# Attention with packed keys and a softplus feed-forward on one core: one subtraction of the weight conversion moves from VectorE to GpSimd

## The chip, the cores and the metric

The kernel runs on one core of one Trainium2 chip. The metric is the device time of an execution in microseconds (us), as a median over runs. The core's engines run side by side, each through its own instruction list in order, and meet through semaphores: TensorE (PE in the profile), VectorE (DVE), ScalarE (ACT), GpSimd (POOL) and SyncE (SP), which issues the DMA transfers.

## The reference

There are eight batches of eight heads, 576 tokens, head width 64. In each batch and head, 32 "pack" queries attend over the 576 keys and values, and then the 576 queries attend over the 32 packed rows. The result, 4608 x 512, goes through a feed-forward block of width 2048 with a softplus between its two products:

```
s = scale * q @ k.T ; a = softmax(s)            # scale = 1/8, head by head
p_packed = attn(p, k, v)                        # 32 x 64 for each head
x   = attn(q, p_packed, p_packed)               # 576 x 64 for each head
h   = x @ w_in                                  # 4608 x 512 by 512 x 2048
g   = max(h, 0) + log1p(exp(-|h|))              # softplus
out = g @ w_out                                 # 4608 x 2048 by 2048 x 512
```

`w_in` and `w_out` arrive as 64-bit floats; all else is 32-bit.

## The kernel before, in words

**The feed-forward products.** Each big product is done with a high and a low word for both factors, as three matmuls: high by high, high by low, low by high. For one batch `b` and one slice `f` of 128 of the 2048 hidden columns, `gemm1` (L497) makes the hidden values in two PSUM tiles `ph` of 288 tokens. `softplus` takes them through ScalarE (|h|, exp, log: L523, L524, L525 into `e`), VectorE (the sum with max(h, 0): L528), GpSimd (L534, 64 left-over tokens into `rest`), and VectorE again (`gh` and `gl`, the high and low words: L513, L514). Two slices later `gemm2_tile` (L541) multiplies them with `wo_h` and `wo_l`, the high and low words of `w_out`. One slice of one batch is called a unit here; batch 0 is units 0 to 15. Only two `ph` tiles and two `e` tiles exist, so TensorE can start the next unit's L497 only when VectorE's L528 has read the old `ph`.

**Attention** of the next batch is cut into small steps and threaded between these matmuls: transposes on TensorE whose results ScalarE copies out of PSUM (`T_k`, `T_q` at L245, `a1T` at L286), scores (L252), VectorE's softmax parts (L327 to L343), and the high and low words of the attention weights (`at_h` L442, `at_l` L443). `make_m` (L460, tiles `psm`, for each second slice of batch 0) multiplies the packed rows with two slices of `w_in`; ScalarE and VectorE split its result into `mh` and `ml` (L475, L476). These small PSUM tiles share two banks in turn, so the second half of an L460 group can begin only when the copy out of the tile before it but one has been made.

**The weight conversion** (`convert`) turns the 64-bit weights into 32-bit ones while batch 0 runs. There are 32 elements of 128 x 512 numbers; elements 4p and 4p+1 are slices 2p and 2p+1 of `w_in`, 4p+2 and 4p+3 the same slices of `w_out`. Each element takes two ScalarE passes (`m` L174, `r` L178), two on VectorE (`t`: L180, L185) and an integer add on GpSimd (L193). For `w_in` that add writes the weight where it is used. For `w_out` it writes back into `t`; ScalarE then rounds it to the high word `wo_h` (L212), and the line of the change makes the low word `wo_l = t - wo_h` (L218). There are two buffers for each of `t` and `r` and one for `m` once batch 0's units run, so element n+2 reuses the `t` of element n: for a `w_out` element that `t` comes free when L218 has read it.

**What sets the order.** TensorE's list stands as the code writes it. The lists of the other engines are arranged by a scheduler ahead of time, so that a changed engine for one operation also moves others around it. On the chip each list is then worked off strictly in order.

Of the kernel before, what the change touches and what calls it, by code (L numbers as in the profile page):

```python
# [26 lines left out]
def pack_attention_then_softplus_ffn(  # L27
# [10 lines left out]
    nc = tc.nc  # L38
# [87 lines left out]
    def load64(srcs, nm, tag="x"):  # L126
        pool, bufs = (cv, 2) if tag == "x" else (work, 1)
        x = pool.tile([P, CN], I64, tag=tag, name=f"x_{nm}", bufs=bufs)
        n = P // len(srcs)
        for i, src in enumerate(srcs):  # L130
            nc.sync.dma_start(
                x[i * n:(i + 1) * n].rearrange("x (a n) -> x a n", a=src.shape[1]), src
            )
        return x
# [13 lines left out]
    def convert(order):  # L148

        srcs = {"i": w_in_src, "o": w_out_src}

        slots = ["x", "x", "at_h", "at_l"]
        xs, ts, rs = {}, {}, {}

        def prefetch(n):
            if n < len(order):
                w, i = order[n]
                xs[n] = load64(srcs[w](i), f"{w}{i}", slots[n % 4] if n < 8 else "x")  # L160

        def first(n):
            x = xs.pop(n)
            lo = x.bitcast(U32).rearrange("x (n two) -> x n two", two=2)[:, :, 0]
            hi = x.bitcast(F32).rearrange("x (n two) -> x n two", two=2)[:, :, 1]
            pool, tm, tr, tt = (work, "gh", "gl", "gh") if spare and n % 2 else (cv, "m", "r", "t")

            m = pool.tile([P, CN], F32, tag=tm, name=f"m_{n}", bufs=LAG + 1 if pool is work else 1)
            nc.scalar.mul(m, hi, 2.0**-112)  # L174


            r = pool.tile([P, CN], I32, tag=tr, name=f"r_{n}", bufs=LAG + 1 if pool is work else 2)
            nc.scalar.activation(r, lo, AF.Copy, scale=2.0**-29)  # L178
            t = pool.tile([P, CN], I32, tag=tt, name=f"t_{n}", bufs=LAG + 1 if pool is work else 2)
            nc.vector.tensor_scalar(t, m.bitcast(I32), -0x80000000, None, op0=ALU.bitwise_and)  # L180
            ts[n], rs[n] = (t, m), r

        def second(n):
            t, m = ts[n]
            nc.vector.scalar_tensor_tensor(  # L185
                t, m.bitcast(I32), 3, t, op0=ALU.logical_shift_left, op1=ALU.bitwise_or
            )
            w, i = order[n]
            dst, a = t, 1
            if w == "i":  # L190
                dst, a = w_in_sb.bitcast(I32)[:, :, i * P:(i + 1) * P], DM // P
            v = [y.rearrange("x (a n) -> x a n", a=a) for y in (t, rs.pop(n))]
            nc.gpsimd.tensor_tensor(  # L193
                dst if a > 1 else dst.rearrange("x (a n) -> x a n", a=a), *v, op=ALU.add
            )

        for n in range(2):
            prefetch(n)
        yield
        for n in range(2, 4):  # L200
            prefetch(n)
        yield
        for n in range(len(order) + 1):
            if n < len(order):
                first(n)
                if n < 6 or n >= 8:
                    prefetch(n + 4 if n < 6 else n + 2)
            yield
            w, i = order[n - 1] if n else ("i", 0)
            t = ts.pop(n - 1)[0].bitcast(F32) if n else None  # L210
            if w == "o":
                nc.scalar.copy(wo_h[:, i, :], t)  # L212
            yield
            if n < len(order):
                second(n)
            yield
            if w == "o":
                nc.vector.tensor_tensor(  # L218
                    wo_l[:, i, :], t, wo_h[:, i, :].bitcast(F32), op=ALU.subtract
                )  # L220
                yield
# [370 lines left out]

    pt = load_pack(0, (nc.sync, nc.scalar))
    conv = convert(order)
    for g in range(G):
        load("k", 0, g)
# [104 lines left out]
```

## Time and profile before

| What | Value |
|---|---|
| time, median of 3 runs | 799.0 us (796.33, 799.0, 799.79) |
| profiled execution, first to last instruction | 794.2 us |
| what lies around that span, by the median | 4.8 us |
| TensorE busy | 766.6 us, 97% of the span |
| VectorE, ScalarE, GpSimd busy | 511.3, 464.8, 94.2 us |
| conversion's work on the three engines | from 12.9 to 138 us of the span |
| L218, the line of the change | 16 instructions on VectorE, 12.5 us together |

The page gives no separate time for the profiled execution itself, so its span stands beside the median. A row of a group names line, engine, operation, output and inputs with shapes and count; then busy time and mean of one; then idle time of the engine just before, and what ended it. A row of a timeline has start, duration, engine, line, operation, and in brackets the engine's idle time before it with what ended that. In a row of windows each engine's busy time is followed by the number of its instructions, and the granted clock of TensorE is a share of full speed.

### The profile page before, as it was taken

The page shows a single profiled execution, that of the slowest core. Times are in us where ns is not written, and L with a number is a line of the kernel's source. Part 1 is how long each engine was busy: PE and PEld are TensorE (multiplying, and loading weights), DVE is VectorE, ACT ScalarE, POOL GpSimd, SP SyncE. Part 2 cuts the span into 40 slices and gives each one's busy share as a digit, 9 for nine tenths or more (in the row PEclk, how much of TensorE's full clock was granted, in tenths as well). Part 3 has the DMA queues.
Part 4 walks back from the last instruction along what each step waited for, and adds up shares of the span by engine and source line. Part 5 has one row for each costly group of instructions (what it writes and reads, how often), then busy time and mean ns, then how long its engine had stood idle before and what let it go on. Part 6 is the DMA issues. An engine that isn't in the chain of part 4 may idle for free.

```text
span 794.2 us, 14986 instructions
## 1 busy us (share of the span) xinstructions
PE 766.6 (97%) x5724; PEld 609.0 (77%) x5724; DVE 511.3 (64%) x1168; ACT 464.8 (59%) x1181; POOL 94.2 (12%) x166
## 2 busy tenths in 40 slices
PE   6879988999999999999999999999999999999997
PEld 4656766877788787877788787887888777778886
DVE  2788899754686547765677447764677546765554
ACT  5769887665662755665554555665555465555540
POOL 1415353000000000000000000000000000000010
PEclk9999999999999999999999999999999999999999
DMA  9977784031213121032213112132211210010002
GB/s 229 248 188 178 172 229 112 8 107 31 61 31 83 45 56 48 18 83 61 61 31 84 26 50 60 31 84 61 61 31 42 56 31 2 1 54 1 1 0 67
DMA packets 38216, 56.02 MB, mean 71 GB/s; under 512 B 4864, under 2 KB 31488, under 8 KB 38144
## 3 DMA queue, kind: packets, MB, share of 16 engines
q1 hardware_dynamic: 37600, 54.93, 27.2%
q8 instruction: 45, 0.74, 0.4%
q14 instruction: 27, 0.22, 0.1%
q10 hardware_dynamic: 544, 0.13, 0.1%
HBM read 45.61 MB, written 9.44 MB: 69 GB/s over the span
## 4 chain that ended last, share of the span: by engine, by line
PE 80%; ACT 0%; DVE 0%; issue 0%; ACTq 0%; DVEq 0%
PE acc L541 40%; PE ph L497 23%; PE acc_m L541 6%; PE psm L460 3%; PE ps L252 2%; PE psT_q L239 2%; PE psT_k L239 2%; PE psp L295 1%; PE psa L285 1%; PE psx L308 0%; PE ppt L105 0%; ACT e L525 0%; ACT e L524 0%; ACT e L523 0%; DVE o L550 0%; DVE o_m L550 0%
## 5 line engine op out<-in xcount | busy, mean ns | idle before, releaser
L528 DVE SCALAR_TENSOR_TENSOR e<-ph,e 128x288 f32<-128x288 f32 x256 | 114.5, 454 | 167.5 <-ACT e L525 166.2
L541 PE MATMUL acc<-wo_h,gh 128*128 128x512 f32 x512 | 214.8, 419 | 0.7 <-DVE o L550 0.7
L541 PE MATMUL acc<-wo_l,gh 128*128 128x512 f32 x512 | 201.6, 394 | 0.0
L541 PE MATMUL acc<-wo_h,gl 128*128 128x512 f32 x512 | 201.5, 394 | 0.0
L523 ACT ACTIVATE e<-ph 128x288 f32<-128x288 f32 x256 | 103.0, 403 | 163.1 <-PE ph L497 110.7
L497 PE MATMUL ph<-at_h,mh 128*128 128x288 f32 x512 | 159.0, 311 | 5.4 <-DVE e L528 4.5
L497 PE MATMUL ph<-at_l,mh 128*128 128x288 f32 x512 | 152.2, 297 | 1.4 <-DVE at_l L443 1.2
L497 PE MATMUL ph<-at_h,ml 128*128 128x288 f32 x512 | 152.2, 297 | 0.0
L497 PEld LDWEIGHTS ph<-at_h,mh 128*128 128x128 f32 x512 | 96.8, 189 | 40.0 <-DVE gl L514 14.1
L534 POOL COPY rest<-e 128x64 f32<-128x64 f32 x128 | 47.3, 369 | 599.3 <-DVE e L528 598.5
L541 PEld LDWEIGHTS acc<-wo_h,gh 128*128 128x128 f32 x512 | 96.4, 188 | 23.1 <-issue 9.8
L541 PEld LDWEIGHTS acc<-wo_h,gl 128*128 128x128 f32 x512 | 96.4, 188 | 21.7
L524 ACT ACTIVATE e<-e 128x288 f32<-128x288 f32 (+1 forms) x240 | 109.2, 455 | 3.5
L525 ACT ACTIVATE e<-e 128x288 f32<-128x288 f32 (+1 forms) x240 | 109.7, 457 | 2.0
L541 PEld LDWEIGHTS acc<-wo_l,gh 128*128 128x128 f32 x512 | 96.9, 189 | 9.8
L497 PEld LDWEIGHTS ph<-at_l,mh 128*128 128x128 f32 x512 | 97.0, 189 | 4.5 <-DVE at_l L443 2.3
L497 PEld LDWEIGHTS ph<-at_h,ml 128*128 128x128 f32 x512 | 96.9, 189 | 0.0
L514 DVE TENSOR_TENSOR gl<-e,gh 128x512 fp32r<-128x512 f32 x128 | 88.0, 688 | 6.9 <-DVE gh L513 0.5
L513 DVE CAST gh<-e 128x512 fp32r<-128x512 f32 x128 | 57.8, 452 | 6.2
L475 ACT CAST mh<-psm 128x512 fp32r<-128x512 f32 (+1 forms) x72 | 35.5, 541 | 41.2 <-PE psm L460 40.8
L476 DVE TENSOR_TENSOR ml<-psm,mh 128x512 fp32r<-128x512 f32 (+1 forms) x72 | 42.7, 622 | 21.8 <-ACT mh L475 21.7
L460 PE MATMUL psm<-w_in_sb,pt 64*32 64x512 f32 (+1 forms) x576 | 38.6, 553 | 6.3 <-ACT T_q L245 2.1
(75 smaller groups left out, 816.7 us busy)
## 6 DMA issues: line engine op xcount, KB each, us to landing
k<-in_k SPq DMA_DIRECT2D x16, 576.0 KB, 4.6
v<-in_v SPq DMA_DIRECT2D x16, 576.0 KB, 4.5
q<-in_q SPq DMA_DIRECT2D x16, 576.0 KB, 4.9
x_i<-in_moe_w_in SPq DMA_DIRECT2D x32, 256.0 KB, 5.9
x_o<-in_moe_w_out SPq DMA_DIRECT2D x16, 512.0 KB, 3.7
out<-o SPq DMA_DIRECT2D x24, 192.0 KB, 2.5
out<-o SPq DMA_DIRECT2D x16, 128.0 KB, 2.4
out<-o SPq DMA_DIRECT2D x24, 64.0 KB, 2.8
```

The costliest lines, as they stand in the source:

```text
L460: nc.tensor.matmul(ps[hh * J:(hh + 1) * J, :n], res["pt"][g][o:o + D, hh * J:(hh + 1) * J], w_in_sb[o:o + D, hh, c * n:(c + 1) * n], start ...
L475: nc.scalar.copy(mh[:, cols], ps[:, :n])
L476: nc.vector.tensor_tensor(ml[:, cols], ps[:, :n], mh[:, cols].bitcast(F32), op=ALU.subtract)
L497: nc.tensor.matmul(ph[:, :C], x[:, ms], y[:, g, cs], start=(i == 0), stop=(i == 3 * G - 1),)
L513: nc.vector.tensor_copy(hi, x)
L514: nc.vector.tensor_tensor(lo, x, hi.bitcast(F32), op=ALU.subtract)
L523: nc.scalar.activation(es[c], hv[c], AF.Abs)
L524: nc.scalar.activation(e[:, x], e[:, x], AF.Exp, scale=-1.0)
L525: nc.scalar.activation(e[:, x], e[:, x], AF.Ln, bias=1.0)
L528: nc.vector.scalar_tensor_tensor(es[c], hv[c], 0.0, es[c], op0=ALU.max, op1=ALU.add)
L534: nc.gpsimd.tensor_copy(rest[:, rest_at(b, f), r:r + REST], e[:, NT * P:])
L541: nc.tensor.matmul(acc, x[:, cs], y[:, f, :], start=(first and i == 0), stop=(last and i == 2),)
```

## The change

`nc.vector.tensor_tensor` at L218 becomes `nc.gpsimd.tensor_tensor`, with the same operands and operation. All 16 low words of `w_out` are now made by GpSimd.

```diff
@@ -215,7 +215,7 @@
                 second(n)
             yield
             if w == "o":
-                nc.vector.tensor_tensor(
+                nc.gpsimd.tensor_tensor(
                     wo_l[:, i, :], t, wo_h[:, i, :].bitcast(F32), op=ALU.subtract
                 )
                 yield
```

TensorE's list stays as it was; VectorE's loses 16 instructions and GpSimd's gains 16; on VectorE and ScalarE many neighbours change places. In the names below the first number after `t_`, `m_`, `r_` is the conversion's element.

GpSimd's list around elements 18 and 19, slices 8 and 9 of `w_out` (units 5 and 6 of batch 0), before and now:

```order
 L193 TENSOR_TENSOR w_in_sb_87<-t_17_1093,r_17_1091 128x4x128
 L534 COPY rest_90<-e_0_5_1078 128x64
 L193 TENSOR_TENSOR t_18_1117<-t_18_1117,r_18_1115 128x512
+L218 TENSOR_TENSOR wo_l_89<-t_18_1117,wo_h_88 128x512
 L193 TENSOR_TENSOR t_19_1198<-t_19_1198,r_19_1196 128x512
+L218 TENSOR_TENSOR wo_l_89<-t_19_1198,wo_h_88 128x512
 L534 COPY rest_90<-e_0_6_1178 128x64
```

The subtraction for element 18 now stands between the adds of elements 18 and 19 on one engine, and it needs `wo_h` from ScalarE in between.

ScalarE's list at the same place, in unit 6:

```order
+L174 ACTIVATE m_19_1194<-x_o9_1095 128x512
 L523 ACTIVATE e_0_6_1178<-ph_0_6_1_1171 128x288
-L174 ACTIVATE m_19_1194<-x_o9_1095 128x512
+L212 CAST wo_h_88<-t_18_1117 128x512
 L524 ACTIVATE e_0_6_1178<-e_0_6_1178 128x576
 L245 COPY T_q_1_0_0_1192<-psT_q_1_0_0_1188 128x288
 L525 ACTIVATE e_0_6_1178<-e_0_6_1178 128x576
-L212 CAST wo_h_88<-t_18_1117 128x512
+L212 CAST wo_h_88<-t_19_1198 128x512
 L286 COPY a1T_1_1_1214<-psa_1_1_0_1215 96x384
```

Before, the copy `a1T` (L286) stood ahead of the second `wo_h`; now it stands behind it.

ScalarE's list in unit 1, around element 10 (slice 4 of `w_out`):

```order
 L524 ACTIVATE e_0_1_728<-e_0_1_728 128x576
+L174 ACTIVATE m_10_751<-x_o4_681 128x512
+L525 ACTIVATE e_0_1_728<-e_0_1_728 128x576
 L245 COPY T_k_1_0_3_769<-psT_k_1_0_3_765 128x288
-L525 ACTIVATE e_0_1_728<-e_0_1_728 128x576
-L174 ACTIVATE m_10_751<-x_o4_681 128x512
```

The pass `m` of element 10 has moved ahead of unit 1's logarithm; on VectorE the passes L180 and L185 of element 10 likewise stand ahead of unit 1's L528 now, where they stood behind it.

## The prediction

> **What bounds the kernel now.** I read the page first: busy shares, slices, chain.
>
> ```profile
> PE 766.6 (97%) x5724; PEld 609.0 (77%) x5724; DVE 511.3 (64%) x1168; ACT 464.8 (59%) x1181; POOL 94.2 (12%) x166
> PE   6879988999999999999999999999999999999997
> ...
> PE 80%; ACT 0%; DVE 0%; issue 0%; ACTq 0%; DVEq 0%
> ```
>
> TensorE is the bound almost everywhere; the reader is to see that its only dips are in the first seven slices of 20 us and in the last. Next come the windows. The conversion's adds and subtractions run from 14 to 138 us; I take 20:146, and a late stretch beside it.
>
> ```profile
> 20.00:146.00 126.00, 109.89 (x921) 84.10 (x918) 108.79 (x244) 96.77 (x207) 48.88 (x45) 0.96 0.72 177
> 300.00:700.00 400.00, 400.00 (x3017) 318.88 (x3016) 256.81 (x607) 229.57 (x615) 26.64 (x71) 1.00 0.17 46
> ```
>
> The columns are PE, PEld, DVE, ACT, POOL, then the granted clock. From 300 to 700 us TensorE never stops, so nothing done by the conversion can shorten or lengthen it. From 20 to 146 us TensorE stands idle for 126.0 - 109.9 = 16.1 us, VectorE is busy for 86%, and the clock is below 1. The change can act only on these 16.1 us, on new gaps beside them, and on the clock. Third, what ended TensorE's idle time there:
>
> ```profile
> PE ph L497 <- DVE e L528: 4.5, 4, 2.3
> PE psm L460 <- ACT T_q L245: 2.1, 1, 2.1
> PE psm L460 <- ACT a1T L286: 1.9, 1, 1.9
> PE psm L460 <- DVE a L319: 1.4, 1, 1.4
> PE ph L497 <- DVE at_l L443: 1.2, 1, 1.2
> ...
> ACT wo_h L212 <- POOL t L193: 8.4, 9, 1.9
> ```
>
> VectorE ended 4.5 + 1.4 + 1.2 = 7.1 us of it, ScalarE's copies 4.0 and more, GpSimd none directly; but ScalarE, the last row says, waited for GpSimd's adds for 8.4 us. A relief of VectorE thus has a few microseconds to win, and a later ScalarE as much to lose.
>
> **The change part by part.** Removed from VectorE and added to GpSimd:
>
> ```profile
> L218 DVE TENSOR_TENSOR wo_l<-t,wo_h x16: 673/684/1731, 24.3 to 137.5; 128x512 fp32r<-128x512 f32 x16
> L193 POOL TENSOR_TENSOR t<-t,r 128x512 int32<-128x512 int32 x16 | 23.8, 1488 | 21.1 <-DVE t L185 14.0 <-ACT e L525 3.1 <-ACT wo_h L212 1.8
> L193 POOL TENSOR_TENSOR w_in_sb<-t,r 128x512 int32<-128x512 int32 x16 | 22.8, 1428 | 58.0 <-DVE t L185 31.4 <-ACT a L272 12.9 <-ACT a1T L286 7.0
> ```
>
> VectorE loses 16 x 0.684 = 10.9 us (the median, free of waits). No subtraction of floats on GpSimd is in this trace. Its nearest row is the integer add on the same shape, 1.43 to 1.49 us; I take 1.46, so 16 x 1.46 = 23.4 us more on an engine busy for 48.9 of 126 us. The bounds are 0.68 us (as on VectorE) and 1.8 us (the longest add seen).
>
> The engines also hold each other up:
>
> ```profile
> 80.18 1.29 POOL L193 TENSOR_TENSOR w_in_sb<-t,r 128x512 int32<-128x512 int32 x1 [2.89 <-DVE t L185]
> 80.30 1.73 DVE L218 TENSOR_TENSOR wo_l<-t,wo_h 128x512 fp32r<-128x512 f32 x1
> ...
> 104.59 0.68 DVE L218 TENSOR_TENSOR wo_l<-t,wo_h 128x512 fp32r<-128x512 f32 x1
> 104.81 1.62 POOL L193 TENSOR_TENSOR t<-t,r 128x512 int32<-128x512 int32 x1 [1.03 <-DVE t L185]
> ```
>
> A VectorE instruction that begins inside a GpSimd add ends only after it: 1.73 us in place of 0.68, 0.56 us past the add's end at 81.47. The other way round the add takes 1.62. Two groups show how often. First L180, all of it and its mean between 20 and 146 us; then L513, between 20 and 146 us and in the whole span:
>
> ```profile
> L180 DVE TENSOR_SCALAR t<-m x32: 367/427/1025, 12.9 to 131.5; 128x512 int32<-128x512 int32 x32
> L180 DVE TENSOR_SCALAR t<-m 128x512 int32<-128x512 int32 x30 | 15.4, 514 | 5.5 <-ACT m L174 4.2 <-POOL w_in_sb L193 0.5 <-ACT r L178 0.5
> ...
> L513 DVE CAST gh<-e 128x512 fp32r<-128x512 f32 x15 | 9.6, 637 | 0.0
> ...
> L513 DVE CAST gh<-e 128x512 fp32r<-128x512 f32 x128 | 57.8, 452 | 6.2
> ```
>
> The excess is 30 x (0.514 - 0.427) = 2.6 us and 15 x (0.637 - 0.452) = 2.8 us, 5.4 us for 32 adds, 0.17 each. Sixteen more take 2.7 us of VectorE's 10.9 back, so it is relieved by about 8 us in 126, if GpSimd's new work meets it no oftener. The Trainium skill, Perfetto Trace Analysis, section Optimizing Scalar/DVE Operations, warns that the two engines share an SBUF port, so that offloading between them might not help; the trace agrees as far as the 1.73 us shows.
>
> The larger part is the handshake. For each pair of w_out slices GpSimd's list was add, add; now it is add, subtract, add, subtract, and the first subtract waits for ScalarE's wo_h. Queued behind it are the second add, behind that the second wo_h, and behind that whatever ScalarE's list holds. I followed the new lists with the old durations through every pair. Three places carry a cost.
>
> *Place A, elements 6 and 7, the way to the first L497.*
>
> ```profile
> 35.66 1.27 POOL L193 TENSOR_TENSOR t<-t,r 128x512 int32<-128x512 int32 x1 [1.16 <-DVE t L185]
> ...
> 37.30 0.44 DVE L328 TENSOR_TENSOR a<-a,m 128x288 f32<-128x288 f32 x1
> ...
> 38.02 0.68 DVE L218 TENSOR_TENSOR wo_l<-t,wo_h 128x512 fp32r<-128x512 f32 x1
> ...
> 39.23 0.45 DVE L328 TENSOR_TENSOR a<-a,m 128x288 f32<-128x288 f32 x1
> ...
> 47.34 0.40 PE L497 MATMUL ph<-at_l,mh 128*128 128x288 f32 x1 [1.20 <-DVE at_l L443]
> ```
>
> After the add that ends at 36.93 GpSimd rested; now both subtractions run there, to about 40, just where VectorE's softmax begins. The first L328 is held to 38.4 (+1.1), the second for another 0.5, and 0.6 is saved by the L218 that is gone: VectorE, full from here to the attention weights, is 1.0 later, and with it TensorE at about 47. **A = +1.0**, bounds -0.6 (no hold) and +2.3 (two full holds, 2 x 1.46 - 0.6).
>
> *Place B, element 10, unit 1.*
>
> ```profile
> 55.34 0.69 ACT L524 ACTIVATE e<-e 128x576 f32<-128x576 f32 x1
> ...
> 55.82 1.27 POOL L193 TENSOR_TENSOR w_in_sb<-t,r 128x512 int32<-128x512 int32 x1 [2.35 <-DVE t L185]
> ...
> 56.93 0.82 DVE L528 SCALAR_TENSOR_TENSOR e<-ph,e 128x288 f32<-128x288 f32 x2 [1.19 <-ACT e L525]
> ...
> 57.44 0.40 PE L497 MATMUL ph<-at_h,mh 128*128 128x288 f32 x1 [2.31 <-DVE e L528]
> ```
>
> L180 and L185 of element 10 now stand ahead of L528. L180 waits for m (to 56.35, behind the exp) and then for the add's end at 57.09; it and L185 take until about 58.05, and L528, which began at 56.93, begins there. TensorE waits for just this: **B = +1.1**, bounds 0 and +2.0 (L185 held as well).
>
> *Place D, elements 18 and 19, unit 6.*
>
> ```profile
> 87.62 1.29 POOL L193 TENSOR_TENSOR t<-t,r 128x512 int32<-128x512 int32 x1 [2.10 <-DVE t L185]
> ...
> 90.07 1.29 POOL L193 TENSOR_TENSOR t<-t,r 128x512 int32<-128x512 int32 x1 [1.15 <-ACT e L525]
> ...
> 90.35 0.50 ACT L286 COPY a1T<-psa 96x384 f32<-96x384 f32 x1
> ...
> 90.76 0.78 PE L460 MATMUL psm<-w_in_sb,pt 64*32 64x256 f32 x16
> ...
> 91.39 0.62 ACT L212 CAST wo_h<-t 128x512 fp32r<-128x512 f32 x1 [0.54 <-POOL t L193]
> ...
> 97.58 0.40 PE L497 MATMUL ph<-at_h,mh 128*128 128x288 f32 x1 [0.97 <-DVE e L528]
> ```
>
> The first add ends at 88.91; wo_h to 89.5; VectorE's L185 of element 19 holds GpSimd to 89.9; the subtraction to 91.2; the second add to 92.5; the second wo_h to 93.1; and a1T, now behind it, to 93.5 where it was done at 90.85. The second half of L460 needs a1T's bank: it ends at 94.0, not 91.5, +2.5 us. The next gap, 0.97 at 97.58, is then covered, because L528 there moves less (+1.0). **D = +1.5**, bounds 0 and +2.5.
>
> The other five pairs, followed in the same way, come out between +0.8 (a later t_24) and -0.4 (a1T ahead of 79.30), together taken as 0, between -1.5 and +1.5: VectorE's relief pays there for later wo_h.
>
> *The clock.*
>
> ```profile
> 58.00:61.00 3.00, 3.00 (x12) 2.84 (x12) 2.60 (x5) 1.57 (x5) 1.78 (x2) 0.50 1.00 253
> ...
> 118.00:122.00 4.00, 3.87 (x22) 3.36 (x23) 4.00 (x9) 2.48 (x8) 1.67 (x1) 0.66 0.67 143
> ```
>
> After the gaps of 2.31 us (at 57.44) and 2.1 us (T_q, ended at 118.13) the granted clock fell to 0.50 and 0.66 for 3 to 4 us, about 1.4 us lost each; after the 1.90 behind a1T at 79.30 it did not. D's new gap would add 1.4; the one before 118.13 may shrink below 2 us and give 1.4 back. I take 0, bounds -1.4 and +2.8. The Trainium skill, TensorE: Matmul & The Clock Gate, Part 1, puts the drop after an idle window of about 3.4 us; by that D would cost no clock. The trace shows drops after shorter gaps.
>
> **Sum:** 1.0 + 1.1 + 1.5 + 0 + 0 = +3.6 us on the span, 794.2 + 3.6 = 797.8; with the 4.8 us by which the median of the three runs stands above the span, 802.6 us. All bounds together would be -3.5 and +11.1.
>
> **The rivals.** *The handshake bites at more places (slower).* One mechanism: ScalarE's second wo_h of a pair waits for add, wo_h, subtract, add. For it: ScalarE already waited for GpSimd here, and the chain grows by 0.62 + 1.46 = 2.1 us a pair. Against it: several lists have m and r moved ahead to fill that time. It decides once the second add ends more than about 1.4 us after ScalarE reaches that wo_h, with a copy for L460 or a logarithm behind it. D in full with its clock (3.9), A and B (2.1), and two more pairs at 1.0 each make +8.0: 807 us.
>
> *The slack takes it (no change).* TensorE's 16.1 us of gaps absorb later work, as at 97.58, and what VectorE gains it loses to the port: 799 us. For it: conversion runs ahead of its use in most pairs; against it: A and B lie on gaps that are already waits for VectorE.
>
> *VectorE's relief wins (faster).* If a subtraction on GpSimd is near its lower bound of 0.68 us and rarely meets VectorE, 10.9 us come off an engine 86% busy that ended 7.1 us of gaps; half of that, with the clock's 1.4, gives -5: 794 us. Against it: the L528 gaps follow ScalarE's logarithm, not a full VectorE.
>
> **How the numbers follow.** Forecast 0.45, slower rival 0.25, no change 0.18, faster rival 0.12. Half a per cent, 4.0 us, is about what a measurement of this kernel can tell from no change: below 795.0 is faster, above 803.0 slower. The forecast, 802.6, lies just inside; of its own range, 799.5 to 805.5, I count 0.17 of 0.45 above 803. Slower 0.25 + 0.17 = 0.42; faster 0.10 of the faster rival's 0.12; the remaining 0.48 is no change. The range is 796 to 808: it takes in the slower rival's price and leaves out the faster rival's and the far bounds.
>
> **What would show it.** L218 rows on GpSimd near 1.46 us; L193, L218, L193, L218 in turn with idle time ended by wo_h; L460 near 92 to 94 us with a gap of 2 us or more ended by a1T; L497 of unit 2 waiting above 3 us for L528; VectorE's busy time about 8 us less. From 150 us on everything should be the old rows, shifted. The forecast is wrong if a1T no longer ends a wait in unit 6, if L218 takes under 1 us, or if TensorE's gaps before 146 us come to under 16 or over 24 us.

## The result, and the profile after

The change is slower. The median went from 799.72 us (17 runs) to 805.86 us (17 runs), a ratio of 1.0078 with a 95% interval of 1.0056 to 1.0100; measured once more at the end of the study, 799.36 to 806.19 us, 1.0086 (1.0058 to 1.0114). That is 6.1 to 6.8 us, inside the range of the prediction and 3.3 us above its time. The profiled execution of the change took 805.81 us, 804.0 of them between its first and last instruction.

From the page of the changed kernel, the busy times:

```profile
PE 775.2 (96%) x5724; PEld 614.1 (76%) x5724; DVE 510.0 (63%) x1152; ACT 466.1 (58%) x1181; POOL 113.7 (14%) x182
```

VectorE lost 16 instructions that had taken 12.5 us, and its busy time fell only from 511.3 to 510.0 us (511.6 to 511.5 in second profiles). That is the first surprise. The windows of the changed kernel, the same two stretches as before:

```profile
20.00:146.00 126.00, 110.23 (x865) 83.64 (x866) 99.26 (x207) 92.61 (x197) 67.47 (x59) 0.89 0.71 177
300.00:700.00 400.00, 400.00 (x3055) 319.61 (x3054) 253.26 (x598) 228.79 (x612) 25.72 (x70) 1.00 0.18 47
```

Late in the program nothing changed: TensorE never stops. In the conversion's stretch it is as busy as before (110.2 us against 109.9) but issued 865 instructions in place of 921, at a granted clock of 0.89 in place of 0.96. The clock over this stretch moves between executions: second profiles of the two kernels have 0.93 for the change and 0.92 for before. The groups of the conversion over the whole span of the changed kernel:

```profile
L218 POOL TENSOR_TENSOR wo_l<-t,wo_h 128x512 fp32r<-128x512 f32 x16 | 22.6, 1417 | 9.0 <-ACT wo_h L212 9.0
...
L212 ACT CAST wo_h<-t 128x512 fp32r<-128x512 f32 x16 | 9.9, 620 | 15.5 <-POOL t L193 15.5
```

A subtraction takes 1.42 us on GpSimd; it waits 9.0 us in all for `wo_h`, and `wo_h` waits 15.5 us for GpSimd's adds, where it waited 8.4. What ended TensorE's idle time from 20 to 146 us:

```profile
PE ph L497 <- DVE e L528: 3.8, 2, 3.4
PE psm L460 <- ACT T_q L245: 2.2, 1, 2.2
PE psm L460 <- ACT a1T L286: 1.8, 2, 1.5
PE ps L252 <- ACT T_q L245: 0.9, 2, 0.7
```

The longest wait is now 3.4 us, and two waits of L252 for ScalarE's `T_q` are in the list (0.9 us; 2.2 in the second profile of the change). L528's row, 4.5 us before, is 3.8 here but 6.4 in that second profile, so VectorE's direct share did not reliably shrink.

**Step by step.** The start of the first L497 of each unit gives the length of each unit. In us, with a second profile of each kernel (named "again"):

| from unit to unit | before | before again | change | change again | mean difference |
|---|---|---|---|---|---|
| 1 to 2 | 4.67 | 4.66 | 5.76 | 5.76 | +1.10 |
| 2 to 3 | 7.83 | 7.76 | 8.93 | 8.94 | +1.14 |
| 3 to 6 | 20.31 | 21.73 | 19.95 | 20.32 | -0.88 |
| 6 to 7 | 5.89 | 5.89 | 7.89 | 7.90 | +2.00 |
| 7 to 8 | 6.11 | 5.77 | 6.48 | 6.47 | +0.54 |
| 9 to 10 | 5.50 | 5.50 | 7.05 | 7.06 | +1.56 |
| 10 to 12 | 14.79 | 14.80 | 16.35 | 15.70 | +1.23 |
| 12 to 14 | 13.67 | 13.66 | 13.68 | 14.48 | +0.42 |
| 1 to 16, all steps | 96.44 | 97.45 | 103.71 | 104.42 | +7.1 |

Units 8 to 9 and 14 to 16 are alike to 0.1 us, and from unit 16 on the work is only shifted. Where unit 1 begins (52.77, 54.03; 54.62, 54.97 us) differs from run to run in every kernel of this study, by up to 4 us, for the most part with the moment at which the transfer of `q` lands (the first transposes of `q` begin between 29.95 and 32.79 us); the difference there is not counted in the table, and place A below comes back to it. The median of before lies 3 to 4 us above its first profile, so the two profiles differ by more (9.8 us) than the medians.

The same work in both kernels, unit 1 to 16, of before and then of the change:

```profile
52.77:149.21 96.44, 86.40 (x676) 65.59 (x676) 84.57 (x183) 78.03 (x166) 38.89 (x38) 0.96 0.60 155
```

```profile
54.62:158.33 103.71, 91.93 (x676) 68.35 (x676) 84.20 (x171) 79.13 (x166) 54.49 (x50) 0.93 0.55 144
```

TensorE's 676 instructions take 5.5 us longer and its idle time grows from 10.0 to 11.8 us; in the second profiles they take 2.3 us longer (87.91 to 90.24) and the idle time grows from 9.5 to 14.2. In the first profiles part of the longer busy time is the clock (0.96 to 0.93). In the second profiles the clock is the same (0.95), so those 2.3 us are not the clock's; that they are short waits which the profile counts as busy is likely, but not shown. VectorE has 12 instructions less here and is busy for 84.20 us against 84.57.

### The profile page after: what moved, and what is told of

Its sections match the earlier page's. It is cut to its first block, busy times and chain, and to the rows that moved or that the text cites. A ratio compares the mean times of both kernels' runs of the same rounds, so it can differ in the third digit from the quotient of the medians.

```text
span 804.0 us, 14995 instructions
## 1 busy us (share of the span) xinstructions
PE 775.2 (96%) x5724; PEld 614.1 (76%) x5724; DVE 510.0 (63%) x1152; ACT 466.1 (58%) x1181; POOL 113.7 (14%) x182
## 4 chain that ended last, share of the span: by engine, by line
PE 79%; ACT 0%; DVE 0%; issue 0%; ACTq 0%; DVEq 0%
PE acc L541 40%; PE ph L497 23%; PE acc_m L541 6%; PE psm L460 3%; PE ps L252 2%; PE psT_q L239 1%; PE psT_k L239 1%; PE psp L295 1%; PE psa L285 1%; PE psx L308 0%; PE ppt L105 0%; ACT e L525 0%; ACT e L524 0%; ACT e L523 0%; DVE o_m L550 0%; DVE o L550 0%
## 5 line engine op out<-in xcount | busy, mean ns | idle before, releaser
L528 DVE SCALAR_TENSOR_TENSOR e<-ph,e 128x288 f32<-128x288 f32 x256 | 114.5, 455 | 174.3 <-ACT e L525 174.2
L497 PE MATMUL ph<-at_h,mh 128*128 128x288 f32 x512 | 159.4, 311 | 6.5 <-DVE e L528 5.4
L497 PE MATMUL ph<-at_l,mh 128*128 128x288 f32 x512 | 152.4, 298 | 0.6 <-DVE at_l L443 0.6
L497 PE MATMUL ph<-at_h,ml 128*128 128x288 f32 x512 | 152.7, 298 | 0.0
L497 PEld LDWEIGHTS ph<-at_h,mh 128*128 128x128 f32 x512 | 97.2, 190 | 41.2 <-DVE gl L514 14.5
L497 PEld LDWEIGHTS ph<-at_l,mh 128*128 128x128 f32 x512 | 97.4, 190 | 3.3 <-DVE at_l L443 1.1
L497 PEld LDWEIGHTS ph<-at_h,ml 128*128 128x128 f32 x512 | 97.4, 190 | 0.0
L514 DVE TENSOR_TENSOR gl<-e,gh 128x512 fp32r<-128x512 f32 x128 | 92.0, 719 | 6.5
L513 DVE CAST gh<-e 128x512 fp32r<-128x512 f32 x128 | 58.2, 454 | 6.8 <-PE ps L252 0.5
L460 PE MATMUL psm<-w_in_sb,pt 64*32 64x512 f32 (+1 forms) x576 | 41.0, 564 | 5.0 <-ACT T_q L245 2.2
```

The lines of the kernel that those rows point to most:

```text
L460: nc.tensor.matmul(ps[hh * J:(hh + 1) * J, :n], res["pt"][g][o:o + D, hh * J:(hh + 1) * J], w_in_sb[o:o + D, hh, c * n:(c + 1) * n], start ...
L497: nc.tensor.matmul(ph[:, :C], x[:, ms], y[:, g, cs], start=(i == 0), stop=(i == 3 * G - 1),)
L513: nc.vector.tensor_copy(hi, x)
L514: nc.vector.tensor_tensor(lo, x, hi.bitcast(F32), op=ALU.subtract)
L528: nc.vector.scalar_tensor_tensor(es[c], hv[c], 0.0, es[c], op0=ALU.max, op1=ALU.add)
```

## Experiments

Two theories stood at the start. The **handshake theory** (the prediction's): the subtraction waits for `wo_h` on GpSimd, and the second add and the second `wo_h` of a pair are queued behind it. The **load theory**: 16 more instructions on GpSimd hold VectorE and delay the conversion, whatever they wait for. Two more came up on the way: that a dropped clock makes the loss (**clock theory**), and that the cost comes from the new order into which the scheduler put ScalarE's and VectorE's work (**order theory**).

**Without the wait.** The change, with a subtraction that does not read `wo_h`. The low words of `w_out` are zero in this kernel; the lists of TensorE, VectorE and ScalarE are those of the change.

```diff
-wo_l[:, i, :], t, wo_h[:, i, :].bitcast(F32), op=ALU.subtract
+wo_l[:, i, :], t, t, op=ALU.subtract
```

> The change, but the subtraction on GpSimd reads t twice (t - t) and not wo_h, so it needs nothing from ScalarE; the low words of w_out become zero. TensorE's, VectorE's and ScalarE's lists are those of the change, row for row; on GpSimd each subtraction now stands right behind its own add. Handshake theory (GpSimd waits for wo_h between the two adds of a pair): the wait is gone, about 9 us of GpSimd's idle time with it, and the time falls most of the way back, ratio to before 1.000 to 1.003. Load theory (GpSimd's 22.6 us of new work holds up VectorE and the second add, whoever waits): stays at 1.007 to 1.009. List theory (the scheduler's new places on ScalarE and VectorE cost the time): stays at 1.007 to 1.009 as well; unit 2's gap stays above 3 us.

Measured: 806.10 us, ratio 1.0077 (1.0049 to 1.0105). Units 1 to 2 and 6 to 7 are 1.08 and 1.76 us longer than before. GpSimd in unit 6 of this kernel, then TensorE's wait:

```profile
90.55 1.28 POOL L193 TENSOR_TENSOR t<-t,r 128x512 int32<-128x512 int32 x1 [2.01 <-ACT e L523]
91.91 1.11 POOL L218 TENSOR_TENSOR wo_l<-t 128x512 fp32r<-128x512 f32 x1
93.71 1.28 POOL L193 TENSOR_TENSOR t<-t,r 128x512 int32<-128x512 int32 x1 [0.69 <-DVE t L185]
```

```profile
96.07 0.64 PE L460 MATMUL psm<-w_in_sb,pt 64*32 64x256 f32 x8 [1.28 <-ACT a1T L286]
```

The subtraction starts as soon as the add has ended, the second add waits for VectorE and not for it, and TensorE still waits for `a1T`. So the wait for `wo_h` is not what costs most of the time. The equal medians say less than they seem to, though. This profile loses 1.58 us in units 14 to 15 to a low clock, as neither profile of the change does; its units 9 to 10 are 0.98 us longer than before where the change's are 1.56; and its subtractions are shorter (1.11 us against 1.42). From unit 1 to 16 it is 7.6 us longer than before, 6.1 without units 14 to 15, against 7.1 in the change: about 1 us may be the wait's.

**The load alone.** The kernel before, with its subtractions on VectorE, and 14 more on GpSimd whose results are overwritten later. ScalarE's and VectorE's lists are those of before.

```diff
+if i + 2 < NF: nc.gpsimd.tensor_tensor(wo_l[:, i + 2, :], t, t, op=ALU.subtract)
```

> Before, with the subtraction still on VectorE, and 14 additional subtractions t - t on GpSimd, one behind each w_out add, which write a slice of wo_l that VectorE overwrites two elements later; nothing waits for wo_h on GpSimd. VectorE's and ScalarE's lists are those of before, row for row. Load theory: GpSimd gets nearly the new load of the change and VectorE is not relieved, so ratio 1.007 or more. Handshake theory and list theory: within 0.3% of before (up to 2.5 us for VectorE's longer holds).

Measured: 804.34 us, ratio 1.0073 (1.0045 to 1.0101). Neither step of the change is there (4.66 and 5.88 us), but the time is lost elsewhere: units 7 to 8 +0.9, 11 to 12 +2.6. How, in unit 11, on GpSimd, on VectorE and on TensorE of this kernel:

```profile
124.06 1.79 POOL L193 TENSOR_TENSOR t<-t,r 128x512 int32<-128x512 int32 x1
125.92 1.10 POOL L221 TENSOR_TENSOR wo_l<-t 128x512 fp32r<-128x512 f32 x1
```

```profile
124.74 1.39 DVE L513 CAST gh<-e 128x512 fp32r<-128x512 f32 x1
126.05 1.29 DVE L339 TENSOR_TENSOR a<-a,z 128x288 f32<-128x288 f32 x1
...
128.26 0.38 DVE L476 TENSOR_TENSOR ml<-psm,mh 128x256 fp32r<-128x256 f32 x1
```

```profile
128.69 0.51 PE L239 MATMUL psT_q<-ident,q 96*128 96x96 f32 x3 [2.33 <-DVE ml L476]
```

L513 and L339 begin inside a GpSimd instruction and end just after it (126.13 against 125.85, 127.34 against 127.02): 1.39 us where this line's mean was 0.64 in the same stretch of before, and 1.29 where L339's mean over the whole of before is 0.45. `ml`, behind them, is late, and TensorE waits 2.33 us for it. So GpSimd's work can cost nearly as much as the change did with no new order at all. It is not a measure of the change's load: this kernel also keeps VectorE's 16 subtractions, and its 14 on GpSimd are shorter (1.10 us).

**Half of it.** Only the even, or only the odd slices on GpSimd; ScalarE's order stays that of before but for an exchange.

```diff
-nc.vector.tensor_tensor(
+(nc.gpsimd if i % 2 == 0 else nc.vector).tensor_tensor(     # even; odd: if i % 2
```

> Only the first w_out slice of each pair (even slices) is subtracted on GpSimd, eight in all; ScalarE's list stays as before but for one exchange in unit 13. In five of the eight pairs the subtraction stands between the two adds, so the handshake is there; the second is on VectorE. Handshake theory: a large part of the cost, ratio 1.004 to 1.007. List theory: about 1.000, since ScalarE's list is that of before. Load theory: half, 1.004.

> Only the second w_out slice of each pair (odd slices) is subtracted on GpSimd, eight in all, behind both adds; ScalarE's list stays as before but for one exchange in unit 3. No subtraction stands between the adds of a pair. Handshake theory: about 1.000, at most 1.002, or a little faster, since VectorE loses 5.5 us of work. List theory: about 1.000. Load theory: half, 1.004, as for the even slices.

Measured: even 800.12 us, 1.0004 (0.9987 to 1.0021); odd 803.48 us, 1.0055 (1.0030 to 1.0080). No theory had foretold both. In the profile of the odd slices unit 1 to 2 took 6.12 us, 1.46 more than before, although the gap inside it, 2.19 us, is no longer than the 2.31 of before. What grew is the matmuls' own time, 3.93 us against 2.36, at a clock that was low from the unit's start:

```profile
56.82:62.94 6.12, 3.93 (x18) 3.73 (x18) 3.45 (x9) 4.76 (x11) 1.50 (x2) 0.71 0.41 108
```

The other 2 us lie in units 10 to 14. Why the odd slices cost and the even do not was not settled.

**GpSimd's order.** The change, with GpSimd's list in the order in which the code writes it: both adds of a pair first, then both subtractions.

```diff
-with tc.manual_schedule(engines={mybir.EngineType.PE}):
+with tc.manual_schedule(engines={mybir.EngineType.PE, mybir.EngineType.Pool}):
```

> The change with GpSimd's list in the order in which the code writes it: in each pair the second add now stands ahead of the first subtraction (add, add, subtract, then the next pair's first add, subtract). VectorE's list is that of the change, ScalarE's but for one exchange in unit 2. Queue theory (the second add is late because the first subtraction is ahead of it, whether or not that waits; so the second wo_h and the a1T behind it are late): unit 6 to 7, 2.0 us longer than before in the change, is back within 0.7 us of before, and the ratio falls to 1.002 to 1.005. List theory (places on ScalarE and VectorE): unit 1 to 2 stays 1.1 us longer; if it explains all, the ratio stays at 1.007 to 1.009. Load theory: 1.007 to 1.009.

Measured: 805.55 us, 1.0096 (1.0075 to 1.0117). Units 6 to 7 shrink to 7.08 us (7.89 in the change). With the gap behind `a1T` at 0.69 us the clock then stays full, and units 7 to 8 shrink to 4.90 (6.48). From unit 6 to 8 this kernel takes 11.98 us, where before takes 11.83 (mean of two) and the change 14.4: the second add's place behind the subtraction costs some 2.4 us there, the clock's part included. But units 1 to 2 grow to 7.59 (5.76), where a subtraction on GpSimd runs beside L514 and L180 and these take 1.44 and 1.49 us, and units 10 to 14 take 3.4 us more than before (1.65 in the change). An order that is better in unit 6 is worse elsewhere.

**The clock.** Extra transposes on TensorE, whose results nobody reads: 16 more at the start in both kernels, and in unit 2's gap 26 in the change, 16 in before. The fill of the change; that of before has 16 in place of 26:

```diff
-            busy(50, "q")
+            busy(66, "q")
+            if (b, f) == (0, 2):
+                busy(26, "gap", (ps_acc, "acc"))
```

> The change with 26 more idle transposes on TensorE ahead of unit 2's first L497 (about 3.0 us, where it stood idle for 3.4) and 66 in place of 50 ahead of the first query transposes (2.4 us of a 3.3 us gap). All other lists are those of the change. Clock theory (gaps of 2 us and more cost 1 to 1.5 us each afterwards through the granted clock): no low clock after unit 2's start and a shorter one from 30 us on; unit 2 to 3 falls from 8.9 to 7.8 us; 1.1 to 2.5 us less than the change, ratio 1.005 to 1.007. If the clock costs nothing on the path: as the change, 1.008.

> Before with 16 idle transposes ahead of unit 2's first L497 (1.8 us of a 2.3 us gap) and 66 in place of 50 ahead of the first query transposes. All other lists are those of before. Clock theory: no low clock after unit 2's start, unit 2 to 3 from 7.8 to about 7.0 us, and the start less disturbed; ratio 0.996 to 0.999, a version that beats both. Otherwise 1.000; if the transposes are in the way, up to 1.002.

Measured: the change 806.03 us, 1.0100 (1.0079 to 1.0121), before 798.07 us, 1.0005 (0.9987 to 1.0024). The windows after the gap at unit 2, of the change and of the filled change, and a wait of the latter:

```profile
60.40:66.40 6.00, 6.00 (x37) 4.66 (x37) 3.79 (x5) 3.30 (x7) 4.92 (x5) 0.72 1.03 210
```

```profile
60.80:66.80 6.00, 4.79 (x37) 3.30 (x37) 3.86 (x5) 3.15 (x7) 4.92 (x5) 1.00 1.01 199
...
67.52 0.47 PE L239 MATMUL psT_k<-ident,k 96*128 96x96 f32 x3 [1.89 <-ACT a L261]
```

With the clock at full speed TensorE is done sooner, and then waits 1.89 us for ScalarE: units 2 to 3 took 8.95 us, as in the change (8.93). The clock is not what sets the end there.

The kernel before, profiled again beside them, served as a yardstick for noise (798.43 us, span 796.7):

> Before, unchanged, profiled again, to see how much of the start (unit 0 at 42.46 us in the first profile, where the other kernels' profiles show 44.4 to 46.2) moves from one execution to the next with the arrival of q. If the start is the change's doing: unit 0 again at 42 to 43 us. If it is the arrival of q: 43 to 47 us, with the first query transposes as late as in the other profiles (30.2 to 32.8 us against 29.95), and units 1 to 16 as far apart as in the first profile.

**Order against load.** Slices 2 and 3 alone on GpSimd give ScalarE's list of the change but for two rows; the other 14 there leave ScalarE's list as before, except for exchanges in units 3, 12 and 13. VectorE's list follows less closely: by the rows of the traces, that of two slices differs from the change's in units 5, 7, 9 and 11 to 14, and that of fourteen differs from before's in units 3, 5, 9 and 11 to 14.

```diff
-nc.vector.tensor_tensor(
+(nc.gpsimd if i in (2, 3) else nc.vector).tensor_tensor(    # two slices
+(nc.gpsimd if i >= 4 else nc.vector).tensor_tensor(         # twelve
+(nc.gpsimd if i not in (2, 3) else nc.vector).tensor_tensor( # fourteen
```

> The kernel before with only two of the sixteen subtractions, those of w_out slices 2 and 3 (elements 6 and 7), on GpSimd. That alone makes the scheduler put the later work of ScalarE in the order that it has in the change (two rows differ), while 14 of the 16 subtractions stay on VectorE. Order theory (what costs is the new order on ScalarE and VectorE, not the work on GpSimd): ratio to before 1.005 to 1.008, unit 1 to 2 about +1.1 us, unit 6 to 7 about +2 us, as in the change. Load theory (what costs is GpSimd's longer list of instructions, which hold VectorE and delay the adds): 2 of 16 subtractions cost an eighth of the change's 0.78%, ratio 1.000 to 1.002, no step of +1 us at units 1 to 2 and 6 to 7.

> The kernel before with twelve of the sixteen subtractions, those of slices 4 to 15, on GpSimd; ScalarE's order stays that of before except for exchanges in units 3, 12 and 13. Order theory: ratio 1.000 to 1.003, unit 1 to 2 and unit 6 to 7 as before. Load theory: 12 of 16 of the change's price and all of its part after unit 3, ratio 1.005 to 1.007, with the lost time at the pairs from unit 4 on.

> The kernel before with fourteen of the sixteen subtractions on GpSimd, all but those of w_out slices 2 and 3 (elements 6 and 7), which alone change ScalarE's order. ScalarE's order stays that of before but for exchanges in units 3, 12 and 13. Sum theory (the new order and the work on GpSimd cost about the same and add up): the change's 0.78% less the 0.16% of the two slices alone, ratio 1.004 to 1.007. Meeting theory (neither costs much alone; the price comes from the change's order and the alternation of add and subtraction on GpSimd together): 1.000 to 1.003, as with slices 4 to 15. Unit 1 to 2 as in the kernel before in both.

> The change once more, on the chip and beside the runs of the kernel before that the run with fourteen subtractions has: ratio 1.006 to 1.010 by every theory. A second profile of it tells which of its steps repeat: B (unit 1 to 2, +1.1 us) and the longer unit 2 to 3 (+1.1) should by the order theory, being in one list; D (6 to 7, +2.0) and 9 to 10 (+1.55) should by the meeting theory as well; the start before unit 1 should not.

Measured: two slices 801.24 us, 1.0016 (0.9989 to 1.0042); twelve 800.60 us, 1.0021 (0.9990 to 1.0051); fourteen 801.75 us, 1.0033 (1.0012 to 1.0054); all sixteen once more 1.0086. The order theory had 1.005 or more for two slices, which lies outside the interval: the order alone is wrong. The load theory had 1.005 for twelve, which the interval just touches; it foretold no step at units 1 to 2 with two slices, and there the steps below speak against it. Fourteen, at 1.0033, lie between what a plain sum (1.004 to 1.007) and a price only of both together (1.000 to 1.003) had foretold, and the interval leaves both. By steps ("order" is ScalarE's), each less the mean of the two profiles of before:

| from unit to unit | two slices (new order) | fourteen (old order) | change, mean of two |
|---|---|---|---|
| 1 to 2 | +1.09 | +0.02 | +1.10 |
| 2 to 3 | +1.14 | +0.53 | +1.14 |
| 3 to 6 | -1.27 | -0.65 | -0.88 |
| 6 to 7 | +1.37 | +0.30 | +2.00 |
| 7 to 8 | -1.02 | -0.05 | +0.54 |
| 9 to 10 | +0.75 | +0.45 | +1.56 |
| 10 to 12 | +0.08 | +1.66 | +1.23 |
| 12 to 14 | +0.34 | +0.10 | +0.42 |
| 1 to 16 | +2.6 | +2.3 | +7.1 |

With two subtractions moved, the steps of unit 1 to 2 and 2 to 3 are there in full: they belong to the order alone, since both subtractions are over before unit 1 begins. In unit 6 the order gives two thirds; its rows in the kernel with two slices:

```profile
93.98 0.62 ACT L212 CAST wo_h<-t 128x512 fp32r<-128x512 f32 x1 [0.68 <-POOL t L193]
94.50 0.47 ACT L286 COPY a1T<-psa 96x384 f32<-96x384 f32 x1
...
95.02 0.64 PE L460 MATMUL psm<-w_in_sb,pt 64*32 64x256 f32 x8 [0.88 <-ACT a1T L286]
```

and in the change, where a subtraction stands between the two adds:

```profile
94.24 1.26 POOL L193 TENSOR_TENSOR t<-t,r 128x512 int32<-128x512 int32 x1
95.54 0.62 ACT L212 CAST wo_h<-t 128x512 fp32r<-128x512 f32 x1 [1.32 <-POOL t L193]
96.06 0.47 ACT L286 COPY a1T<-psa 96x384 f32<-96x384 f32 x1
96.58 0.64 PE L460 MATMUL psm<-w_in_sb,pt 64*32 64x256 f32 x8 [1.50 <-ACT a1T L286]
```

The gap grows from 0.88 to 1.50 us, and in the next unit the clock differs. Two slices, then the change:

```profile
95.60:100.50 4.90, 4.90 (x32) 4.19 (x29) 3.51 (x9) 4.47 (x10) 1.62 (x1) 1.00 0.69 168
```

```profile
97.20:103.60 6.40, 6.40 (x32) 5.50 (x29) 3.11 (x8) 4.66 (x10) 2.21 (x4) 0.73 0.42 112
```

The same 32 matmul records take 4.90 us at full clock and 6.40 at 0.73: 1.5 us that neither the order nor the load costs by itself. The steps of the two parts add up to 4.9 of the change's 7.1 us; 7 to 8 holds 1.6 of the rest, 6 to 7 and 9 to 10 0.3 to 0.4 each. The ratios agree with this (0.16% and 0.33% against 0.78 and 0.86%), but their intervals are too wide to show by themselves that the parts don't simply add. Nor are the parts pure: where VectorE's list differs in the kernel with fourteen, its step can be the order's as well as the load's.

## Why the prediction was right, and where its sizes were wrong

The direction of the forecast (+3.6 us on the span) held, and so did the range; the size was 3 us short. By the prediction's own limits its time, 802.6 us, lay just inside "no change" (up to 803.0), to which it gave 0.48; what came was "slower", to which it gave 0.42. That the total came this near is in part luck: D's second half failed, and the pairs taken as 0 cost about as much as the whole forecast.

**B, +1.1 us, right.** Unit 1 to 2 grew by 1.09 and 1.10 us. The rows of the change show the chain as predicted:

```profile
58.33 0.68 ACT L525 ACTIVATE e<-e 128x576 f32<-128x576 f32 x1
...
58.54 0.69 DVE L180 TENSOR_SCALAR t<-m 128x512 int32<-128x512 int32 x1 [0.94 <-ACT m L174]
59.27 0.69 DVE L185 SCALAR_TENSOR_TENSOR t<-m,t 128x512 int32<-128x512 int32 x1
59.87 0.82 DVE L528 SCALAR_TENSOR_TENSOR e<-ph,e 128x288 f32<-128x288 f32 x2
...
60.38 0.40 PE L497 MATMUL ph<-at_h,mh 128*128 128x288 f32 x1 [3.40 <-DVE e L528]
```

L528 stands ready at 59.01, when the logarithm ends, and begins at 59.87. That it is the order and no subtraction is shown by the kernel with two slices, which has the same +1.09.

**D, the first half right in size, not in cause.** L460 was put 2.5 us later with a gap of 2 us or more behind `a1T`; the step is +2.0 and the gap 1.50. The prediction put it down to add, subtract, add with the wait for `wo_h`. The order alone, `a1T` behind the second `wo_h`, makes 1.37 of it, and without the wait 1.76 remain: the queue on GpSimd counts, the wait in it hardly. **The second half failed:** the next gap was to absorb 1.0. Two slices do that (-1.02 at 7 to 8); the change does not (+0.54), because the clock fell; with both adds ahead of the subtractions, where it did not fall, 7 to 8 is again 1.04 us shorter than before. D with what follows is +2.5 in place of +1.5.

**A, +1.0 us, there at about half its size, and by another path.** The holds of L328 came. VectorE's rows, before again and then the change, in two executions whose first transposes of `q` begin alike, at 30.44 and 30.49 us:

```profile
39.43 0.68 DVE L218 TENSOR_TENSOR wo_l<-t,wo_h 128x512 fp32r<-128x512 f32 x1
40.12 0.46 DVE L336 TENSOR_REDUCE z<-a 128x9 f32<-128x288 f32 x1
40.48 0.45 DVE L328 TENSOR_TENSOR a<-a,m 128x288 f32<-128x288 f32 x1
```

```profile
38.76 0.83 DVE L328 TENSOR_TENSOR a<-a,m 128x288 f32<-128x288 f32 x1
...
39.98 1.05 DVE L328 TENSOR_TENSOR a<-a,m 128x288 f32<-128x288 f32 x1
40.96 0.44 DVE L336 TENSOR_REDUCE z<-a 128x9 f32<-128x288 f32 x1
```

The second L328 ends at 40.93 and at 41.03: the two holds (0.38 and 0.60) fill the place of the L218 that left and of L336. But L336, which stood ahead of that L328, stands behind it now, 0.84 us later. With it the first L497 of unit 0 is 0.80 us later (43.72, 44.52), the last `at_l` 0.50 and unit 1 0.59 (54.03, 54.62). The L497 for which the prediction had worked this out, the one behind the first `at_l`, came 0.36 us earlier (48.60, 48.24), because that `at_l` has another place in the list. The 0.6 us lie ahead of unit 1, outside the 7.1 of the table; one pair of profiles, in a stretch that scatters with the landing of `q`, does not settle the size.

**The other five pairs, taken as 0 (-1.5 to +1.5): the term that was most wrong.** Units 2 to 3 (+1.14), 9 to 10 (+1.56) and 10 to 14 (+1.65), less 0.88 in 3 to 6, make about +3.5. Unit 9 to 10 is the mechanism of the slower rival at one place. ScalarE's rows of before, and then GpSimd's, ScalarE's and TensorE's of the change:

```profile
106.57 0.63 ACT L212 CAST wo_h<-t 128x512 fp32r<-128x512 f32 x1
```

```profile
110.12 1.68 POOL L218 TENSOR_TENSOR wo_l<-t,wo_h 128x512 fp32r<-128x512 f32 x1 [0.35 <-ACT wo_h L212]
111.76 1.47 POOL L193 TENSOR_TENSOR t<-t,r 128x512 int32<-128x512 int32 x1
...
113.26 0.62 ACT L212 CAST wo_h<-t 128x512 fp32r<-128x512 f32 x1 [1.71 <-POOL t L193]
...
116.95 0.38 ACT L245 COPY T_q<-psT_q 128x288 f32<-128x288 f32 x1
...
117.38 0.70 PE L252 MATMUL ps<-T_q,pt 64*32 64x288 f32 x10 [0.71 <-ACT T_q L245]
```

The second `wo_h` did not wait before; now it waits 1.71 us with the exponential, the logarithm and `T_q` behind it. The rival's price of 807 us was nearer than the forecast's, and its mechanism is part of the truth; its wait for `wo_h` is a small part at most (9 to 10 is still 0.98 us longer without it).

**The port, sized far too small.** The prediction let sixteen more GpSimd instructions take 2.7 of 10.9 us back. Over the same work VectorE got next to nothing: 84.57 to 84.20 us, and 84.78 to 84.67 in the second profiles. Its groups between units 1 and 16, before and then the change:

```profile
L180 DVE TENSOR_SCALAR t<-m 128x512 int32<-128x512 int32 x23 | 12.2, 531 | 5.3 <-ACT m L174 4.2 <-POOL w_in_sb L193 0.5 <-ACT r L178 0.5
L514 DVE TENSOR_TENSOR gl<-e,gh 128x512 fp32r<-128x512 f32 x15 | 10.2, 678 | 0.1
L218 DVE TENSOR_TENSOR wo_l<-t,wo_h 128x512 fp32r<-128x512 f32 x12 | 9.7, 809 | 0.1
```

```profile
L180 DVE TENSOR_SCALAR t<-m 128x512 int32<-128x512 int32 x23 | 14.1, 613 | 5.5 <-ACT m L174 5.1
L514 DVE TENSOR_TENSOR gl<-e,gh 128x512 fp32r<-128x512 f32 x15 | 14.1, 939 | 0.2
```

L514 took 3.9 us more and L180 1.9 more; smaller rises in L185 and L339 follow. The mean excess for each add in the kernel before (0.17 us) was the wrong rule for the subtractions: their place in the list, right after `wo_h`, falls on the high and low words of the unit. Before, no L514 began inside a GpSimd add; in the change 4 of 15 began inside an add or a subtraction, and these took 1.66 us each, against 0.68 on average before. The prediction's sentence on the hold is too wide as well: L528 began inside one 16 times in the change and took 0.45 us each, as it does alone. The Trainium skill, Perfetto Trace Analysis, section Optimizing Scalar/DVE Operations, warns that offloading between the two engines might not help because they share an SBUF port; this trace agrees, with 0.4 us won for 9.7 us moved.

**The clock, 0.** Over units 1 to 16 it was 0.96 and 0.95 before, 0.93 and 0.95 in the change. It costs where D's gap grew, and nothing at unit 2, where the filled change shows ScalarE setting the end. The Trainium skill, TensorE: Matmul & The Clock Gate, Part 1, puts the drop after an idle window of some 3.4 us, by which D would have cost no clock; the trace disagrees, with 0.73 after a gap of 1.50 us. What the drops go by is shown at the end.

**What lies around the span.** The prediction added 4.8 us, the median less the span of one execution. It is 1.8 us in the change (805.81 - 804.0) and 1.7 in before (798.43 - 796.7): the first profile was of an execution some 3 us quicker than the median. The sum still came out on the right footing.

**What was to show it.** Seen: L218 at 1.42 us (1.46 taken), add and subtraction in turn, unit 2's wait above 3 us, old rows from unit 16 on. Half seen: the gap behind `a1T` in unit 6, 1.50 us and not 2. Not seen: VectorE's total 8 us lower. TensorE's gaps from 20 to 146 us came to 15.8 us and, in the second profile, 19.2; the bound of 16 that was to count against the forecast is met by the first, since much of the loss lies in TensorE's busy time and in work that has moved past 146 us.

**What stays open.** Why eight even slices cost nothing and eight odd ones 0.55%, how much of the fourteen's +2.3 us is VectorE's new order, and which of the waits inside TensorE's busy time make up its part of the loss.

## What to carry to other kernels

Moving an operation to another engine changes three things: the engine's load, its neighbours' speed, and the order in which a scheduler lays out everything else. Here two of sixteen moved instructions brought nearly the whole new order of ScalarE, and the price of all sixteen, by the steps of the profiles, was about half again the sum of the two parts. Relief of the old engine is to be counted over equal work in the new profile, not from the durations of what left; and a change in two steps should be tried as its two halves before it is judged as one.

## What the runs showed of the hardware that was not expected

GpSimd's instructions gave back to VectorE's neighbours nearly all that left VectorE: it kept 0.4 us of 9.7. Not every instruction is held: in the change all 4 of L514 and all 14 of L180 that began inside a GpSimd add or subtraction ended after it (1.66 and 0.79 us on average, against 0.68 and 0.44 undisturbed), while L528, 16 times inside one, took 0.45 us as alone.

The granted clock after a gap is not told by the gap's length. In six-microsecond windows that begin at the end of a gap of 1.81 us (before again) and of 1.28 us (the change without the wait) it was 0.72; after gaps of 1.90 us (before) and 2.56 us (the load alone) it stayed at 1.00. The prediction had read a bound near 2 us out of one profile; further profiles did not bear it out.

What the profiles show in its place: the clock is either 1.00 or 0.50, and it changes only at the ends of stretches of 3.41 us, whose places differ from run to run (in before, the first and the last change between 30 and 792 us lie 223 such stretches apart). Two stretches of before again, with the gap of 1.81 us in the first:

```profile
77.03:80.44 3.41, 1.60 (x18) 0.76 (x20) 2.75 (x8) 2.68 (x7) 1.35 (x2) 1.00 1.09 264
80.44:83.85 3.41, 3.41 (x18) 2.60 (x19) 3.07 (x7) 2.02 (x6) 1.28 (x1) 0.50 0.63 203
```

and two of the load alone, with the gap of 2.56 us cut in two between them:

```profile
77.80:81.21 3.41, 2.32 (x17) 1.33 (x16) 3.41 (x6) 1.97 (x6) 2.64 (x3) 1.00 1.04 240
81.21:84.62 3.41, 1.93 (x18) 1.52 (x19) 3.41 (x7) 3.08 (x8) 1.72 (x3) 1.00 0.83 181
```

The shorter gap leaves TensorE busy for 1.60 us of its stretch, and the next stretch has half the clock; the longer one leaves it 2.32 and 1.93 us, and the stretch after it is at 1.00 too. Between 45 and 160 us of the 14 profiles there are 407 such stretches at full clock: after all 27 in which TensorE was busy for less than 0.52 of the time the clock fell, after none of the 335 with 0.73 or more, and after 6 of the 45 between. D's gap is a case of it: its stretch was busy for 1.91 us in the change, before the drop, and for 2.54 in the kernel with two slices, where no drop came. The cause inside the chip is not shown by this.
